# Two single banks in place of a joint pair for the experts, a bank's copy on VectorE, and three moves in a hand-written order

## The chip, the core and the metric

One core of a Trainium2 chip runs the whole program. The metric is device time in microseconds (us), the median of several executions. TensorE (PE) does the matrix products and writes them to PSUM, which has eight banks of 128 x 512 fp32; VectorE (DVE), ScalarE (ACT) and GpSimd (POOL) work on the results, and SyncE (SP) issues most of the loads. Each engine takes its instructions strictly in program order, and waits between engines go over semaphores.

## The reference

Attention over 8 batches, 8 heads, 576 positions of 64 (fp32, scores masked by blocks of 64 rows), and a mixture of 8 experts on its output, one expert per token:

```
scores = q @ k.T / 8, masked by blocks;  x = softmax(scores) @ v          # 4608 tokens x 512
logits = x @ w_gate + modality_bias[modality_id];  e = argmax(logits)
out[token] = softmax(logits)[e] * (relu(x[token] @ w1[e]) @ w2[e])        # w1 512x1024, w2 1024x512
```

## The kernel before

**Attention** works on pairs of heads, 32 pairs, four pairs to a batch. `run_slot` walks a table of names, `ORDER`, once for each pair: at slot p, `S0` to `S3` write the scores of pair p+1 (L216), `M0` to `M4` take negated row maxima on VectorE (L220), `E0` to `E4` the exponentials on ScalarE (L226), `T0` to `T2` transpose the exponentials of pair p on PE (L235), `C0` to `C4` copy the transposes from PSUM to the tile `pt` (L249, all on ScalarE), `G` and `H` make the gate's columns (L255, L258), `V` multiplies with the values of pair p-1 (L281), and `D`, `Z0`, `Z1` divide (L296 to L310, VectorE). So the order of every engine's queue is written out by hand, in ORDER; nothing reorders it later.

Scores and transposes use six banks: `bank0` to `bank3` and the two halves of `wide`, one PSUM tile of 1024 columns (`banks[4]`, `banks[5]`); its last row block of scores spans both. The value products go to `o0` and `b0`. Waits are placed by the tile framework from the tiles that instructions read and write; for `wide` one tile name stands for both banks.

**Routing** of a batch starts in the slot after its fourth pair: a list of about 20 small steps (`logits` to `place_sum`, mostly VectorE on 128x72) is popped by the names `q1` to `q6`, `qp` and `qv` in ORDER. Then nine scatters (L406, GpSimd) write the batch's records to DRAM, a VectorE instruction (L405) each.

**The last slot** follows its own table, `LAST`, which mixes the last pair's `V`, `D`, `Z` and the last routing with the first expert products: `+turn0` transposes fetched rows, `+up0` to `+up3` are the first eight products with w1, `+place` issues one scatter behind a pause of POOL (L642), and `+flush` all that are left.

**Experts** then run in blocks of 512 rows: eight `up` products (L754, 128x512 each from 12 matmuls; evicted by L757 on ScalarE and L758 on VectorE into `hidden`, an upper and a lower part), with the first half of the `down` products behind the fourth and the second half at the end (L855). A block has four down results `y`, one per bank of `ys`; `finish` (L862, ScalarE) scales one and a GpSimd scatter writes it out (L863):

```
ys = (o0, banks[5], banks[4], b0)
if nxt is not None:
    (self.turn_third if nxt.parts == THIRD else self.turn_rows)(nxt)
...
for i in range(s.parts):
    self.down(s, i, range(4, 8) if s.parts == WIDE else range(8))
```

`turn_rows` transposes the next block's rows on VectorE (L738), rounds them on ScalarE (L741) and takes the remainder on VectorE (L744, L745). It stands ahead of the second half of the down products, so on ScalarE its four casts are queued ahead of the four `finish` instructions.

Of the kernel before, what the change touches and what calls it, by code (L numbers as in the profile page):

```python
# [11 lines left out]
F32 = mybir.dt.float32  # L12
# [7 lines left out]
PSUM = bass.MemoryType.PSUM  # L20
DRAM = bass.MemoryType.DRAM

B, H, S, D = 8, 8, 576, 64
N, DM, NE, DF = 4608, 512, 8, 1024
NPAIR = B * H // 2
# [39 lines left out]
    ((7, 0), (7, 1), (7, 2), (7, 3)), ((8, 0), (8, 1), (8, 2), (8, 3)), ((6, 3), (4, 2), (2, 1)),  # L65
)
POS = {x: 4 * r + i for r, room in enumerate(ROOMS) for i, x in enumerate(room)}
SUMS = ((2, 4, 6, 5), (1, 3, 7, 8, 0))
TAILS = ((6, 3, 20, 0), (0, 5, 20, 1), (4, 2, 21, 0), (8, 4, 21, 1), (2, 1, 22, 0))
PRODUCTS = tuple(((s,), j) for j in range(4) for s in (6, 7, 5, 8, 4, 3, 2, 1) if s >= 2 * j + 1)  # L70
# [1 line left out]
PARTS = (("idf", (128,)), ("ii", (128,)), ("iom8", (NE,)), ("iom72", (NSUB, NE)), ("first9", (NE, NSUB)), ("base8", (NE,)), ("edges", (N // SLOT,)), ("side", (NSUB,)), ("token", (NSUB,)), ("nth", (N // 128,)), ("few", (2,)), ("half", (1,)))  # L72

ORDER = (
# [3 lines left out]
)  # L78
OPENING = ("S0", "S1", "S2", "S3", "M0", "E0", "M1", "E1", "M2", "E2", "M3", "E3", "M4", "E4")
WARM = {"T1": 3}  # L80
# [4 lines left out]
    (18, "V"): ("chosen", "stage"), (18, "T1"): ("stage",), **{(slot, "T1"): ("restage",) for slot in range(19, 32)}, (20, "L"): ("ids",), (26, "T0"): ("fetch",), (31, "T0"): ("fetch",),  # L85
}
LAST = (
    ("+turn0", 0), ("V", 1), ("+place", 0), ("D", 1), ("+up0", 0), ("+place", 0), ("Z0", 1), ("Z1", 1), ("+steps1", 0), ("+place", 0), ("+up1", 0),
    ("+place", 0), ("+steps10", 0), ("+place", 0), ("+up2", 0), ("+place", 0), ("+steps9", 0), ("+up3", 0), ("+flush", 0),
)  # L90

# [21 lines left out]
def attention_moe(ctx, tc, qk, vr, bkw, mid, mb, w1, w2, cf, ld, out):  # L113
    nc = tc.nc
    pe, act, dve, pool = nc.tensor, nc.scalar, nc.vector, nc.gpsimd

    cst = ctx.enter_context(tc.tile_pool(name="cst", bufs=1, side="left"))
    drm = ctx.enter_context(tc.tile_pool(name="drm", bufs=1, space=DRAM))
    records = drm.tile([2 * NROW, REC], F32, name="records")

    cft = cst.tile([128, cf.shape[1]], F32, name="cf")
    con, off = {}, 0
    for n, shape in PARTS:
        size = int(np.prod(shape))
        v = cft[:, off : off + size]
        con[n] = v.rearrange("p (a b) -> p a b", a=shape[0]) if len(shape) > 1 else v
        off += size
    idf, ii, iom8, iom72, first9, base8, side, token = (con[n] for n in ("idf", "ii", "iom8", "iom72", "first9", "base8", "side", "token"))
    wg = cst.tile([128, PPB, 2 * NE], F32, name="wg")
    scratch = cst.tile([128, 1024], F32, name="scratch")  # L130
# [4 lines left out]
    run = cst.tile([128, NE], F32, name="run")  # L135
# [1 line left out]
    midf = cst.tile([128, 2, B * NSUB], F32, name="midf")  # L137
    mbt = cst.tile([128, 2, NE], F32, name="mbt")
    bias = cst.tile([128, B * NSUB, NE], F32, name="bias")
    cst.tile([128, 32], F32, name="padc")  # L140
    steady = ctx.enter_context(tc.tile_pool(name="steady", bufs=1, side="left"))
    extra = steady.tile([128, 14 * 1024], F32R, name="extra")
    staging = [steady.tile([128, 1024], F32, name=f"staging{i}") for i in range(2)]
    xg0 = steady.tile([128, 1024], F32, name="xg0")
# [9 lines left out]
    ps = ctx.enter_context(tc.tile_pool(name="ps", bufs=1, space=PSUM))  # L154

    banks = [ps.tile([128, 512], F32, name=f"bank{i}") for i in range(4)]
    wide = ps.tile([128, 1024], F32, name="wide")
    banks += [wide[:, 0:512], wide[:, 512:1024]]
    o0, b0 = (ps.tile([128, 512], F32, name=n) for n in ("o0", "b0"))
    xrb.append(att.tile([128, NSUB, REC], F32, name="xr2"))  # L160
    btmp = staging[0][:, 0 : B * NSUB * NE].rearrange("p (a e) -> p a e", e=NE)
    raws = [att.tile([128, 2 * S], F32, name=f"raw{i}") for i in range(2)]
# [74 lines left out]
    def copies(p, c):  # L237
        g, h = c // 2, c % 2
        n = len(GROUPS[g])
        first = min(POS[x] for x in GROUPS[g])  # L240
        if g == 2:
            dst = pairs[p].pt[:, first : first + n].rearrange("p b (h q) -> p h b q", h=2)
            src = wide.rearrange("p (h c) -> p h c", h=2)[:, :, 0 : 64 * n].rearrange("p h (b q) -> p h b q", q=64)
        else:
            dst, src = pairs[p].pt[:, first : first + n, 64 * h : 64 * h + 64], banks[c][:, 0 : 64 * n].rearrange("p (b q) -> p b q", q=64)
        if g == 0:
            dst = pairs[p].pt[:, 0:16, 64 * h : 64 * h + 64].rearrange("p (a b) q -> p a b q", b=4)[:, 0:4:3]
            src = src.rearrange("p (a b) q -> p a b q", a=2)
        act.copy(dst, src)  # L249

    def gates(p):
        for j in range(6):
# [61 lines left out]
    def routing(b):  # L314
# [97 lines left out]

            placing.extend((scatter, i) for i in range(NSUB))

        return [logits, total, total_out, biased, top, shifted, hits, expo, hit_index, first, onehot, counts, weight, counts_out, running, place_run, place_pick, weight_guard, weight_out, place_sum]

    sel = {}

# [81 lines left out]
    def run_slot(slot):  # L500
        nonlocal steps, ex
        for name, stage in LAST if slot == NPAIR else ORDER:
            p = slot - stage
            if placing and slot < NPAIR and name in SPOTS:
                g, c = placing.pop(0)
                g(c)
            for what in EARLY_STEPS.get((slot, name), ()):
                if ex is None:
                    ex = Experts(ctx, tc, cst, scratch, con["edges"], con["nth"], con["few"], con["half"], records, early_reads, scatters, bias, rest, bases, idf, w1, w2, out, sel, run, base8, pick, dot, banks, (o0, banks[5], banks[4], b0), placing, staging, extra, firsts, first, xrb, xg0, pts[0][:, 15:19], lambda kind: any(getattr(f, "kind", "") == kind for f in steps))
                ex.early(what)  # L510
            if name[0:6] == "+steps":
                for f in steps[0 : int(name[6:])]:
                    f()
                steps = steps[int(name[6:]) :]
                continue
            if slot == 0 and name in WARM:
                warm(WARM[name])
            if name[0] == "+":
                ex.early(name[1:])
                continue  # L520
            if name[0] == "q":
                kind = "" if name[1].isdigit() else name
                kinds = (kind,) if kind else ("", "c")
                quick = bool(steps) and getattr(steps[0], "kind", "") == "c"
                for _ in range(1 if kind else 2 * (name != "q6") if quick else 2 if slot in HURRIED else 1 + (len(steps) > 20)):
                    if slot > 1 and steps and getattr(steps[0], "kind", "") in kinds:
                        steps.pop(0)()
                continue
            if not 0 <= p < NPAIR and name not in ("L", "v", "Y"):
                continue  # L530
            if p < NPAIR:
                emit(name, p)
            if name == "Z1" and p % PPB == PPB - 1:
                these = routing(p // PPB)
                steps = these[0:1] + steps + these[1:]
                if p // PPB == EARLY - 1:
                    choose(Later(dve, steps))

    engines = {ET.PE, ET.Activation, ET.DVE, ET.Pool}
    with tc.manual_schedule(engines=engines | {ET.SP}):  # L540
        load(0)
        for _ in range(NWARM):
            pe.matmul(b0, zeros[:, 0:128], zeros, start=True, stop=True)
        nc.sync.dma_start(cft, cf)
        load(1)
        scale(0)
        load_rest()
        for name in OPENING:
            emit(name, 0)
        for slot in range(NPAIR + 1):  # L550
            run_slot(slot)
    with tc.manual_schedule(engines=engines):
        att_stack.close()
        ex.run_all(steps)
# [493 lines left out]
```

## Time and profile before

| | |
|---|---|
| median of 3 runs | 736.71 us (736.17 to 738.45) |
| profiled execution | 742.5 us, its span 740.6 us |
| PE busy | 702.5 us, 95% of the span |
| DVE, ACT, POOL busy | 331.6, 337.3, 216.5 us |
| attention (32 pairs) | to about 293 us of the span |
| expert blocks | from there to the end |

An engine's busy share is an average over both stages. A busy PE is one that has instructions in flight; a gap of it is idle time, and the view names what ended the gap. "granted clock" (PEclk) is the share of TensorE's 2.4 GHz that it was given.

### The profile page before, as it was taken

The page shows a single profiled execution, that of the slowest core. Times are in us where ns is not written, and L with a number is a line of the kernel's source. Part 1 is how long each engine was busy: PE and PEld are TensorE (multiplying, and loading weights), DVE is VectorE, ACT ScalarE, POOL GpSimd, SP SyncE. Part 2 cuts the span into 40 slices and gives each one's busy share as a digit, 9 for nine tenths or more (in the row PEclk, how much of TensorE's full clock was granted, in tenths as well). Part 3 has the DMA queues.
Part 4 walks back from the last instruction along what each step waited for, and adds up shares of the span by engine and source line. Part 5 has one row for each costly group of instructions (what it writes and reads, how often), then busy time and mean ns, then how long its engine had stood idle before and what let it go on. Part 6 is the DMA issues. An engine that isn't in the chain of part 4 may idle for free. (4 is left out here: it accounts for less than half of the span.)

```text
span 740.6 us, 20776 instructions
## 1 busy us (share of the span) xinstructions
PE 702.5 (95%) x8618; PEld 578.5 (78%) x8619; DVE 331.6 (45%) x974; ACT 337.3 (46%) x673; POOL 216.5 (29%) x251
## 2 busy tenths in 40 slices
PE   8999999999999998999599899898999999999996
PEld 5888888788878887888478788787887878878785
DVE  4665767776777786752312322223122132222121
ACT  6888887778888886221221221213113032131211
POOL 2422253545275763799020110201002010020111
PEclk9999999999999999999889999999999999999999
DMA  6555565667676865231741420403407030020100
GB/s 211 168 156 162 170 188 178 192 195 237 192 248 201 274 210 152 60 136 54 144 114 58 85 67 19 114 1 77 149 0 228 1 81 33 0 79 1 50 32 24
DMA packets 52690, 87.78 MB, mean 119 GB/s; under 512 B 10350, under 2 KB 31086, under 8 KB 52592
## 3 DMA queue, kind: packets, MB, share of 16 engines
q1 hardware_dynamic: 46064, 66.90, 33.0%
q0 software_dynamic: 6528, 19.50, 7.3%
q8 instruction: 69, 1.13, 0.6%
q14 instruction: 29, 0.24, 0.1%
HBM read 65.28 MB, written 21.27 MB: 117 GB/s over the span
## 5 line engine op out<-in xcount | busy, mean ns | idle before, releaser
L758 DVE SCALAR_TENSOR_TENSOR extra<-bank,extra 128x512 fp32r<-128x512 f32 (+1 forms) x70 | 46.8, 669 | 263.4 <-ACT extra L757 263.4
L757 ACT ACTIVATE extra<-bank 128x512 fp32r<-128x512 f32 (+1 forms) x70 | 40.7, 581 | 219.6 <-PE bank L754 219.6
L220 DVE TENSOR_REDUCE nm<-bank 128x1 f32<-128x512 f32 (+2 forms) x192 | 85.5, 484 | 62.8 <-PE bank L216 56.5
L406 POOL DMA_INDIRECT records<-xr,pi x72 | 73.5, 1020 | 115.3 <-DVE den L296 47.9
L226 ACT ACTIVATE pm<-bank,nm 128x512 f32<-128x512 f32 (+2 forms) x192 | 91.6, 527 | 27.6 <-DVE nm L220 24.0
L281 PE MATMUL b<-v,pt 64*64 64x73 f32 (+1 forms) x1612 | 97.8, 227 | 0.0
L281 PE MATMUL o<-v,pt 64*64 64x73 f32 (+1 forms) x1488 | 93.5, 228 | 0.3 <-issue 0.3
L216 PE MATMUL bank<-raw 64*64 64x64 f32 (+5 forms) x768 | 93.0, 442 | 0.4 <-DMA raw<-qk 0.4
L281 PEld LDWEIGHTS o<-v,pt 64*64 64x64 f32 (+1 forms) x1488 | 81.6, 135 | 13.1 <-issue 6.5
L281 PEld LDWEIGHTS b<-v,pt 64*64 64x64 f32 (+1 forms) x1612 | 85.1, 136 | 0.2 <-issue 0.2
L249 ACT COPY pt<-bank 128x512 f32<-128x512 f32 x128 | 66.3, 605 | 9.9 <-PE bank L235 8.8
L855 PE MATMUL wide<-extra 128*128 128x512 f32 x216 | 55.5, 412 | 15.4 <-ACT scratch L862 15.4
L855 PEld LDWEIGHTS wide<-extra 128*128 128x128 f32 x216 | 42.6, 199 | 26.2 <-ACT scratch L862 17.1
L216 PE MATMUL wide<-raw 64*64 64x64 f32 (+3 forms) x512 | 58.9, 369 | 1.0 <-ACT pt L249 0.9
L754 PE MATMUL bank<-extra,w0ha 128*128 128x512 f32 (+1 forms) x176 | 59.0, 361 | 0.0
L863 POOL DMA_INDIRECT out<-scratch,ids_b x9 | 8.8, 974 | 164.5 <-ACT scratch L862 163.6
L754 PE MATMUL bank<-extra,w0la 128*128 128x512 f32 (+1 forms) x152 | 56.6, 372 | 0.0
L226 ACT ACTIVATE pm<-wide,nm 128x256 f32<-128x256 f32 (+2 forms) x96 | 43.8, 527 | 20.3 <-DVE nm L220 14.9
L855 PE MATMUL wide<-w1b,extra 128*128 128x512 f32 x192 | 47.0, 397 | 5.9 <-ACT scratch L862 5.9
L754 PE MATMUL bank<-xtl,w0ha 128*128 128x512 f32 x128 | 50.6, 395 | 0.0
L754 PE MATMUL bank<-extra,w0lb 128*128 128x512 f32 x128 | 50.3, 393 | 0.0
L754 PE MATMUL bank<-extra,w0hb 128*128 128x512 f32 x128 | 50.1, 391 | 0.0
(241 smaller groups left out, 1234.7 us busy)
## 6 DMA issues: line engine op xcount, KB each, us to landing
raw<-qk SPq DMA_DIRECT2D x31, 576.0 KB
v<-vr SPq DMA_DIRECT2D x32, 438.0 KB
vt<-qk SPq DMA_DIRECT2D x32, 288.0 KB
xr<-records SPq DMA_DIRECT2D x32, 256.0 KB
staging<-w SPq DMA_DIRECT2D x32, 128.0 KB
staging<-w SPq DMA_DIRECT2D x8, 512.0 KB
plain<-w SPq DMA_DIRECT2D x16, 128.0 KB
plain<-w SPq DMA_DIRECT2D x4, 512.0 KB
```

Source lines behind the costliest of these rows:

```text
L216: pe.matmul(place(s, a, b)[64 * t : 64 * t + 64], d.q[hs, D * s : D * s + D], d.k[hs, a:b], start=True, stop=True)
L220: dve.tensor_reduce(pairs[p].nm[:, s : s + 1], whole(s), AX.X, ALU.max, negate=True)
L226: act.activation(d.pm[:, o : o + D * (s + 1)], whole(s), AF.Exp, bias=d.nm[:, s : s + 1], scale=1.0)
L249: act.copy(dst, src)
L281: pe.matmul(o, d.pt[rows, at, t : t + 64], d.v[rows, h, block, :], start=key not in begun, stop=last)
L406: last = pool.indirect_dma_start(records[:], bass.IndirectOffsetOnAxis(ap=g.pi[i], axis=0), xr[:, i, :], None, bounds_check=2 * NROW - 1, ...
L754: nc.tensor.matmul(hp, w[:, kc, ms], x[:, kc, 0:n], start=i == 0, stop=i == len(mm) - 1)
L757: nc.scalar.activation(hh, hp, AF.Relu)
L758: nc.vector.scalar_tensor_tensor(hl, hp, 0.0, hh, ALU.max, ALU.subtract)
L855: nc.tensor.matmul(y, s.hs[m][x][:, ts], self.part(w, 1, m // 2)[:, m % 2, :], start=first, stop=last)
L863: last = nc.gpsimd.indirect_dma_start(self.out, bass.IndirectOffsetOnAxis(ap=s.list.ids[:, s.t + i : s.t + i + 1], axis=0), yo, None, boun ...
```

## The change

Six edits. The pool that holds `wide` is closed ahead of the last slot, and two tiles of one bank each, `late0` and `late1`, take its place in `banks[4:6]` and in the experts' `ys`. The copy `C1` (bank 1) goes to VectorE. In ORDER, `C1` stands directly behind `C0`, `q2` ahead of `qp`, and `q3` to `q6` behind `E4` (before, `q2` to `q5` stood between the maxima). In the routing list `counts_out` stands ahead of `weight`. In LAST, `+up0` stands ahead of `V`. An unused tile `padc` of 128 x 32 is dropped. Numbers of lines and of tiles differ between the two programs for that reason.

```diff
-    ("Q", -1), ("L", -2), ("V", 1), ("v", -1), ("D", 1), ("Z0", 1), ("Z1", 1), ("T0", 0), ("C0", 0), ("T1", 0), ("C2", 0), ("C1", 0), ("C3", 0),
+    ("Q", -1), ("L", -2), ("V", 1), ("v", -1), ("D", 1), ("Z0", 1), ("Z1", 1), ("T0", 0), ("C0", 0), ("C1", 0), ("T1", 0), ("C2", 0), ("C3", 0),
...
-    ("+turn0", 0), ("V", 1), ("+place", 0), ("D", 1), ("+up0", 0), ("+place", 0), ("Z0", 1), ("Z1", 1), ("+steps1", 0), ("+place", 0), ("+up1", 0),
+    ("+turn0", 0), ("+up0", 0), ("+place", 0), ("V", 1), ("+place", 0), ("D", 1), ("Z0", 1), ("Z1", 1), ("+steps1", 0), ("+place", 0), ("+up1", 0),
...
+    o0, b0 = (ps.tile([128, 512], F32, name=n) for n in ("o0", "b0"))
+    joint = ExitStack()
+    wide = joint.enter_context(tc.tile_pool(name="joint", bufs=1, space=PSUM)).tile([128, 1024], F32, name="wide")
...
-        act.copy(dst, src)
+        dve.tensor_copy(dst, src) if c in ON_DVE else act.copy(dst, src)
...
-        for slot in range(NPAIR + 1):
+        for slot in range(NPAIR):
             run_slot(slot)
+        joint.close()
+        late = ctx.enter_context(tc.tile_pool(name="late", bufs=1, space=PSUM, reuse_waits="tile"))
+        banks[4:6] = [late.tile([128, 512], F32, name=f"late{i}") for i in range(2)]
+        ex.ys = (o0, banks[5], banks[4], b0)
+        run_slot(NPAIR)
```

`ON_DVE` is `(1,)`. On PE, at the second half of the down products of the first block of 512 rows, with the engines that a row waits for in brackets, there stood

```order
L855 MATMUL o_101<-extra 128x512 [waits DVE_49]
L855 MATMUL wide<-extra 128x512 x12
L855 MATMUL wide<-extra 128x512 [waits Activation_49]
L855 MATMUL wide<-extra 128x512 x11
L855 MATMUL b_102<-extra 128x512 x12
```

and now stands

```order
L861 MATMUL o_99<-extra 128x512
L861 MATMUL o_99<-extra 128x512 [waits DVE_49]
L861 MATMUL late_6149<-extra 128x512 x12
L861 MATMUL late_6148<-extra 128x512 x12
L861 MATMUL b_100<-extra 128x512 x12
```

The wait for ScalarE between the second and the third result is no longer there. On VectorE, in a slot of the first batch's routing (`nm` are the maxima), there stood

```order
L310 TENSOR_TENSOR gl<-o_101,inv 128x32
L220 TENSOR_REDUCE nm<-bank_96 128x1
L220 TENSOR_REDUCE nm<-bank_98 128x1 x2
L383 SCALAR_TENSOR_TENSOR cum<-cf,table 128x72
L385 TENSOR_TENSOR pos<-table,run 128x72
L220 TENSOR_REDUCE nm<-bank_97 128x1 x2
L394 TENSOR_TENSOR eq<-cum,pos 128x72
L220 TENSOR_REDUCE nm<-bank_99 128x1
L397 TENSOR_TENSOR eq<-eq,oh 128x72
L398 TENSOR_TENSOR run<-run,cum 128x8
L220 TENSOR_REDUCE nm<-wide 128x1 x3
L380 TENSOR_SCALAR sm<-sm 128x9
```

and the same steps, one slot earlier, now stand behind all maxima, with the new copy ahead of these:

```order
L250 COPY pt_113<-bank_96 128x2x4x64
L221 TENSOR_REDUCE nm<-bank_95 128x1
L221 TENSOR_REDUCE nm<-bank_97 128x1 x2
L221 TENSOR_REDUCE nm<-bank_96 128x1 x2
L221 TENSOR_REDUCE nm<-bank_98 128x1
L221 TENSOR_REDUCE nm<-wide 128x1 x3
L378 TENSOR_REDUCE sm<-ex 128x9
L384 SCALAR_TENSOR_TENSOR cum<-cf,table 128x72
L386 TENSOR_TENSOR pos<-table,run 128x72
L395 TENSOR_TENSOR eq<-cum,pos 128x72
L398 TENSOR_TENSOR eq<-eq,oh 128x72
L399 TENSOR_TENSOR run<-run,cum 128x8
```

The third place is PE at the start of the last slot. The last pair's value products (L281) followed the gate's (b_102) there:

```order
L255 MATMUL b_102<-wg,vt 64x16 x11
L281 MATMUL bank_96<-v_108,pt_112 64x73 [waits DMAHW1_49,Activation_49]
L281 MATMUL bank_96<-v_108,pt_112 64x73
L281 MATMUL bank_97<-v_108,pt_112 64x73 x2
L281 MATMUL bank_96<-v_108,pt_112 64x73 x2
```

Now the products of `+up0` do, which wait for the turned rows, and the value products stand behind them:

```order
L256 MATMUL b_100<-wg,vt 64x16 x11
L760 MATMUL bank_97<-extra,w0ha 128x256 [waits Activation_49,Pool_49]
L760 MATMUL bank_97<-extra,w0la 128x256 [waits Pool_49]
L760 MATMUL bank_97<-extra,w0ha 128x256 [waits DVE_49]
L760 MATMUL bank_97<-extra,w0ha 128x256 [waits Pool_49]
```

What moved there is a whole product group: 24 matmuls with w1 now precede 100 value products. On POOL, the program of before has 18 pauses of L642 and the changed one 12, since the routing of a batch comes to its scatters a slot earlier.

## Rows read from the trace of the kernel before

**Rows 1.** The page: busy time, share of the span and instructions of engines.

```profile
PE 702.5 (95%) x8618; PEld 578.5 (78%) x8619; DVE 331.6 (45%) x974; ACT 337.3 (46%) x673; POOL 216.5 (29%) x251
```

**Rows 2.** Waits, longest first: us in total, times, longest us.

```profile
PE wide L855 <- ACT scratch L862: 21.4, 8, 9.9
```

**Rows 3.** Second to fourth down result: us, PE busy (matmuls), PEclk, DMA share, GB/s.

```profile
358.35:376.37 18.02, 8.16 (x25) 0.72 0.97 186
414.73:423.68 8.95, 7.09 (x26) 0.84 0.64 111
...
693.19:699.82 6.63, 5.85 (x26) 1.00 0.38 121
sum 71.53, PE 50.15; mean PE 6.27
```

**Rows 4.** The same windows at two first halves, undisturbed.

```profile
392.87:398.31 5.44, 5.44 (x26) 1.00 0.64 193
532.24:537.83 5.59, 5.59 (x26) 1.00 0.00 0
```

**Rows 5.** Timeline of the first block of 512 rows: start, us, engine, line.

```profile
357.08 2.03 SPq L725 DMA_DIRECT2D xr<-records  x4
...
365.06 1.30 DVE L738 STREAM_TRANSPOSE xr<-xr 128x512 f32<-128x512 f32 x2 [7.91 <-DMA xr<-records]
...
369.90 0.69 DVE L745 TENSOR_TENSOR xtl<-xr,extra 128x512 fp32r<-128x512 f32 x1
370.36 0.68 ACT L862 ACTIVATE scratch<-wide,both_lead 128x512 f32<-128x512 f32 x1
...
371.09 5.47 PE L855 MATMUL wide<-extra 128*128 128x512 f32 x12 [9.86 <-ACT scratch L862]
```

**Rows 6.** Timeline of POOL and SP ahead of that load: last scatters, then lists.

```profile
348.06 1.53 POOL L642 TENSOR_SCALAR pt<-pt 128x512 f32<-128x512 f32 x1
349.77 1.03 POOL L406 DMA_INDIRECT records<-xr,pi  x1 [0.18 <-issue]
352.28 0.42 SPq L700 DMA_DIRECT2D both_a<-records  x1
```

**Rows 7.** Windows of 4, 13, 13 pairs and one: us, then PE, PEld, DVE, ACT, POOL busy.

```profile
13.20:47.78 34.58, 34.58 (x847) 29.41 (x843) 21.95 (x66) 28.84 (x63) 12.43 (x11) 1.00 0.53 158
47.78:164.62 116.84, 113.84 (x2744) 96.31 (x2743) 82.39 (x309) 94.59 (x205) 43.40 (x39) 1.00 0.59 178
164.62:282.89 118.27, 115.93 (x2745) 97.22 (x2745) 87.90 (x306) 96.05 (x209) 65.17 (x100) 1.00 0.72 222
47.78:55.97 8.19, 8.19 (x211) 7.10 (x211) 6.02 (x21) 6.82 (x17) 1.36 (x2) 1.00 0.51 153
```

**Rows 8.** Lines by form, 13.2 to 282.89 us: busy, mean ns, idle before.

```profile
L249 ACT COPY pt<-bank 128x512 f32<-128x512 f32 x122 | 63.3, 605 | 9.5 <-PE bank L235 8.4 <-PE wide L235 1.1
...
L216 PEld LDWEIGHTS wide<-raw 64*64 64x64 f32 x480 | 24.3, 133 | 11.5 <-ACT pt L249 8.0
...
L220 DVE TENSOR_REDUCE nm<-bank 128x1 f32<-128x512 f32 x30 | 20.7, 692 | 57.2 <-PE bank L216 51.6 <-ACT table L337 4.0 <-PE b L255 1.6
...
L226 ACT ACTIVATE pm<-wide,nm 128x256 f32<-128x256 f32 x30 | 14.3, 476 | 19.4 <-DVE nm L220 14.3 <-DVE pi L405 1.3 <-DVE xr L391 1.0
```

**Rows 9.** Windows on PE at the last slot, and one pair's value products.

```profile
293.25:298.17 4.92, 4.92 (x101) 0.65 1.12 228
276.32:279.64 3.32, 3.32 (x104) 1.00 0.13 47
291.25:311.87 20.62, 17.41 (x209) 0.92 0.37 86
```

**Rows 10.** Timeline of PE in the last slot.

```profile
293.25 4.92 PE L281 MATMUL bank<-v,pt 64*64 64x73 f32 x100 [1.80 <-ACT v L258]
...
304.10 0.39 PE L754 MATMUL wide<-extra,w0ha 128*128 128x256 f32 x1 [1.41 <-DVE extra L758]
```

**Rows 11.** Window on VectorE over one pair's division (D, Z0, Z1).

```profile
207.01:208.57 1.56, 1.49 (x10) 1.00 0.43 88
```

More of the change, by code (lines that the diff above doesn't have):

```diff
@@ L67 @@
 POS = {x: 4 * r + i for r, room in enumerate(ROOMS) for i, x in enumerate(room)}
+ON_DVE = (1,)
 SUMS = ((2, 4, 6, 5), (1, 3, 7, 8, 0))
@@ L139, in attention_moe @@
     bias = cst.tile([128, B * NSUB, NE], F32, name="bias")
-    cst.tile([128, 32], F32, name="padc")
     steady = ctx.enter_context(tc.tile_pool(name="steady", bufs=1, side="left"))
@@ L156, in attention_moe @@
     banks = [ps.tile([128, 512], F32, name=f"bank{i}") for i in range(4)]
-    wide = ps.tile([128, 1024], F32, name="wide")
+    o0, b0 = (ps.tile([128, 512], F32, name=n) for n in ("o0", "b0"))
+    joint = ExitStack()
+    wide = joint.enter_context(tc.tile_pool(name="joint", bufs=1, space=PSUM)).tile([128, 1024], F32, name="wide")
     banks += [wide[:, 0:512], wide[:, 512:1024]]
-    o0, b0 = (ps.tile([128, 512], F32, name=n) for n in ("o0", "b0"))
     xrb.append(att.tile([128, NSUB, REC], F32, name="xr2"))
@@ L413, in place_sum @@
             placing.extend((scatter, i) for i in range(NSUB))
-        return [logits, total, total_out, biased, top, shifted, hits, expo, hit_index, first, onehot, counts, weight, counts_out, running, place_run, place_pick, weight_guard, weight_out, place_sum]
+        return [logits, total, total_out, biased, top, shifted, hits, expo, hit_index, first, onehot, counts, counts_out, weight, running, place_run, place_pick, weight_guard, weight_out, place_sum]
     sel = {}
@@ L508, in run_slot @@
                 if ex is None:
-                    ex = Experts(ctx, tc, cst, scratch, con["edges"], con["nth"], con["few"], con["half"], records, early_reads, scatters, bias, rest, bases, idf, w1, w2, out, sel, run, base8, pick, dot, banks, (o0, banks[5], banks[4], b0), placing, staging, extra, firsts, first, xrb, xg0, pts[0][:, 15:19], lambda kind: any(getattr(f, "kind", "") == kind for f in steps))
+                    ex = Experts(ctx, tc, cst, scratch, con["edges"], con["nth"], con["few"], con["half"], records, early_reads, scatters, bias, rest, bases, idf, w1, w2, out, sel, run, base8, pick, dot, banks, (), placing, staging, extra, firsts, first, xrb, xg0, pts[0][:, 15:19], lambda kind: any(getattr(f, "kind", "") == kind for f in steps))
                 ex.early(what)
```

4 rows, old and new, of the table ORDER are left out of this document.

## The prediction

> **What bounds the kernel now.** I read the page first: PE is busy for 95% of the span, no other engine for half of it [rows 1]. So two things can shorten the program: gaps of PE, and stretches in which it is busy but paced by others. Next the waits: the longest of PE is one kind, products into `wide` that wait for ScalarE's L862, 21.4 us in 8 times, the longest 9.9 [rows 2]. Eight is the number of 512-row blocks, so I measured each of them over windows, from the start of the second down result to the start of the fourth [rows 3]. The eight windows hold 71.53 us. In a first half, where nothing stalls, the same two results take 5.44 us with the first expert's weights and 5.59 us with the second's [rows 4]; four blocks are of either kind, 44.1 us. The excess is **27.4 us**: 12.6 in the first block, 3.5 in the second, about 2 in each of five, 1.0 in the last. It is more than the 21.4 us of idle time, because the granted clock is 0.72 and 0.84 in the first two windows: after a gap PE goes on at 1.2 GHz for a while.
>
> The timeline of the first block shows why PE waits. L862 reads the second result, in one half of `wide`; the third result goes to the other half. The tile framework sees one tile, and lets the third wait for the read of the second. ScalarE comes to that read late, since the four casts of the next block's rows are queued ahead of it, and these wait for rows that land at 365.06: the read starts at 370.36, PE goes on at 371.09 [rows 5]. Nothing in the data asks for that wait.
>
> **The change part by part.**
>
> *Two tiles for the joint pair.* With `late0` and `late1` the third result has no wait in the program's order, nor has the fourth. What is late next? After the fourth result PE needs the next block's turned rows and a bank for the next up product. In the six middle blocks the rows are turned while PE is still in the down products, so nothing replaces the stall. In the first block PE would be through with the fourth result at 358.35 + 2 x 5.44/2 + 2.72 = 366.5, and the turning ends at 369.90 + 0.69 = 370.6 [rows 5]; the first up product, of 12 matmuls in the order of the four parts, would end some 4 us late. But the rows come earlier too. The load at 357.08 follows the lists' loads (352.28), and these the last scatter of POOL at 349.77, the end of a row of 18 pauses of 1.53 us with a scatter of 1.03 each, 2.8 us a step [rows 6]. Only 12 are left in the changed program, so this row could end 6 x 2.8 = 17 us earlier; since the last batch's own nine cannot start before its routing, I take 11. Rows that land near 354 are turned in the shadow of the down products. I take the whole 27.4 us; at the worst, with rows no earlier, 23.4. The last slot has the same false wait once more, 1.41 us at 304.10 [rows 10]; it is in that slot's term.
>
> *The attention pairs.* From score product to score product, 30 pairs take 34.58 + 116.84 + 118.27 = 269.69 us: 8.65 us a pair in the first four, before any routing, 8.99 in the next thirteen and 9.10 in the last thirteen [rows 7]. PE's busy share is 97 to 100%, yet the shortest pair takes 8.19 us with the same products [rows 7]. So PE is busy and paced: matmuls stand in flight behind semaphores. Two rows say which. The loads of scores into `wide` wait for ScalarE's copies 8.0 us, and the exponentials wait for maxima, 14.3 us at `wide`'s alone [rows 8].
>
> (a) C1 to VectorE takes 605 ns [rows 8] from ScalarE's chain C0, C2, C1, C3, C4, so `wide` comes free about 0.5 us earlier; that covers the wait just named (0.27 us a pair), and PE gains no more than it waits. (b) The routing steps behind the maxima let the last exponentials start earlier by the two to five steps that stood between. (c) The copy costs VectorE between ScalarE's 605 ns and its own read of 512 columns, 692 ns [rows 8]; I take 0.69, since that is the same engine and the same bank width. It waits for C0, and lies in the gap ahead of the first maximum, 57.2 us in 30 pairs or 1.9 a pair [rows 8]. Behind the copy queue q1, q2 and that maximum. Without this cover it would cost 0.69 x 30 = 21 us, the lower bound of this term; the upper bound is all pairs at 8.19, 269.69 - 245.7 = 24 us gained.
>
> Between the two I go by VectorE's budget. It is busy 82.39/13 = 6.3 us a pair in the middle stretch and 87.90/13 = 6.8 in the last, where it also scales q [rows 7]; with the copy 7.0 and 7.5. What it must wait for stays: the first maximum for its scores (1.9 less the copy, 1.2). That makes 8.2 and 8.7, plus some 0.2 in pairs where four to six routing steps now stand ahead of the division, which waits for nothing else then, and which gates wait for. I take 8.3, 8.45 and 8.8 us a pair: 34.58 - 33.2 = 1.4, 116.84 - 109.9 = 7.0, 118.27 - 114.4 = 3.9, together **12.2 us**.
>
> The Trainium skill speaks against moving the copy: the page "VectorE: DVE Perf Modes", section "Specifications", places ScalarE closer to PSUM and VectorE closer to SBUF, and its table of op costs ("The TRN2 errata") would make a copy of 512 columns from PSUM an estimated 0.66 us on VectorE against 0.57 on ScalarE. The rows above have the same sign with 692 against 605 ns, and by the page's price the lower bound would be 20 us in place of 21.
>
> *The last slot.* PE waited 1.80 us there, then ran the value products in 4.92 us where another pair's took 3.32, since the granted clock was 0.65, then waited 1.41 us [rows 9, 10]. Now 24 up products stand first. They need rows that VectorE turns behind the previous pair's division, the copy and two scatter indices, so I expect PE to wait about as long, and the lower clock to hit the up products in place of the values. The second wait, 1.41 us, goes. From the gate's end to the first down result it is 20.62 us [rows 9]; I take **1 us** gained, from 3 lost to 5 gained. `counts_out` ahead of `weight` changes the order of two steps of 0.2 to 0.4 us, off PE's path; the dropped tile costs nothing.
>
> **The sum.** 27.4 + 12.2 + 1 = 40.6 us. Against the profiled execution's 742.5 us this makes 702; that execution is 5.8 us above the median, and I take the same gain from the median: 736.7 - 40.6 = **696 us**.
>
> **The rivals.**
>
> *Every pair at its floor.* VectorE's added work is all hidden and each pair takes 8.19 us: 27.4 + 24 + 1, 684 us. For it: in the shortest pair VectorE is busy for only 6.02 of the 8.19 us [rows 7]. Against it: VectorE is idle only 1.65 us a pair in the last stretch once the copy is in.
>
> *VectorE becomes the bound of attention.* The copy and the routing tails land on the division, which gates and the bank's release wait for; the pairs take as long as before or up to 0.69 us more: 708 to 729 us. For it: VectorE's 7.5 us of work in a pair with two fixed waits. Against it: its own gap ahead of the maxima.
>
> *The wait for `wide` only moves*, to rows not yet turned in the first block, and later reads of `late` wait as `wide` did: only attention and the last slot gain, 723 us. The program's order speaks against it, for no row of the third result waits.
>
> *Slower.* The copy stands behind the whole division, 1.56 us [rows 11], which waits for the value products; scores into bank 1 wait for the copy, and the next value products for the scores. If that ring closes, a pair costs the division and the copy more, 1.56 + 0.69 us, 67.5 us in 30 pairs: 736.7 - 28.4 + 67.5 = 776 us. It decides from 28.4/30 = 0.95 us a pair on. Against it: scores reach bank 1 last but one of their pieces, and the division ends before they start.
>
> **How the numbers follow.** The sum has a chance of 0.52 (its own range 690 to 704), every pair at its floor 0.15, VectorE as the bound 0.25, the moved wait 0.03, slower 0.03; 0.02 for no change by mishaps that cancel. I leave out the far end of VectorE's case and the last three: 684 to 713 us. No change means within 0.3%, 2.2 us, about what a measurement of this kernel can tell: 0.02. Slower 0.03, faster 0.95.
>
> **What would show it.** In the changed profile PE has no wait for L862 in the down products, and windows from the second to the fourth result hold 5.44 and 5.59 us with the granted clock at 1.00, also in the first block. The last scatter comes 10 us or more earlier against the first down result. A pair takes 8.3 to 8.8 us; the copy takes 0.6 to 0.7 us on VectorE, and exponentials wait less for maxima. In the last slot PE waits ahead of `+up0`. The prediction is wrong if the pairs' average stays at 9 us or falls to 8.2, or if PE waits for turned rows behind the fourth result.

## The result, and the profile after

The changed kernel takes **699.09 us** (median of 4 runs, 697.74 to 699.53) against 736.59 before (4 runs, 736.17 to 738.45): a ratio of 0.9483, 95% interval 0.9462 to 0.9504, 37.5 us gained. Its profiled execution took 697.74 us, with a span of 695.9. PE is now busy for 97% of it; the row answers to [rows 1]:

```profile
PE 677.0 (97%) x8619; PEld 573.5 (82%) x8619; DVE 350.3 (50%) x1006; ACT 318.6 (46%) x641; POOL 206.9 (30%) x245
```

The waits of PE in the changed kernel, longest first (us in total, times, longest), have none for the `finish` line, which is L868 now:

```profile
PE b L256 <- DVE gl L311: 3.3, 7, 1.0
PE o L374 <- DVE oh L370: 2.8, 3, 1.2
PE o L334 <- DVE l L331: 2.4, 7, 0.7
PE bank L760 <- ACT extra L747: 1.5, 1, 1.5
```

Windows of the changed kernel, with the columns of [rows 7]: the 4, 13 and 13 pairs; the last six of these pairs; the last slot from the gate's end to the first down result; second to fourth down result in the first, the second, the fifth (the first of the second expert) and the last block of 512 rows; and the whole expert part.

```profile
12.98:46.06 33.08, 32.85 (x846) 28.64 (x843) 24.22 (x70) 26.97 (x59) 12.66 (x11) 1.00 0.56 167
46.06:154.83 108.77, 107.02 (x2744) 94.58 (x2743) 89.63 (x327) 86.82 (x193) 44.38 (x39) 1.00 0.65 192
154.83:271.45 116.62, 109.51 (x2749) 97.00 (x2745) 97.05 (x328) 88.66 (x194) 68.66 (x102) 0.99 0.78 230
214.69:271.45 56.76, 51.51 (x1268) 45.47 (x1267) 46.00 (x158) 40.87 (x91) 37.72 (x56) 0.97 0.74 225
279.59:299.03 19.44, 17.32 (x201) 16.52 (x201) 13.51 (x40) 5.96 (x16) 11.72 (x11) 0.91 0.22 65
345.30:350.74 5.44, 5.44 (x25) 4.50 (x24) 3.97 (x7) 3.08 (x6) 0.97 (x1) 1.00 0.25 65
388.82:394.26 5.44, 5.44 (x25) 4.50 (x24) 3.96 (x7) 3.08 (x6) 0.55 (x1) 1.00 0.24 61
...
519.38:524.82 5.44, 5.44 (x25) 4.50 (x24) 3.96 (x7) 3.07 (x6) 0.97 (x1) 1.00 0.27 64
...
649.94:655.38 5.44, 5.44 (x25) 4.50 (x24) 0.00 (x0) 1.37 (x2) 1.94 (x2) 1.00 0.34 99
299.03:690.17 391.14, 390.79 (x1762) 323.90 (x1760) 113.91 (x206) 96.44 (x157) 62.49 (x69) 1.00 0.27 71
```

All eight windows of down results hold 5.44 us, where [rows 3] have 18.02 to 6.63, and the clock is 1.00 in each. The expert part takes 391.1 us; before, from the first down result at 311.87 to the start of the last matmul at 734.93, it took 423.1. Pairs take 8.27, 8.37 and 8.97 us.

The timeline of the changed kernel in the last slot and at the first block of 512 rows answers to [rows 5, 6, 10]. The last scatter of records starts at 322.45, 23.4 us behind the first down result; before, it was 37.9 us behind it. The next rows' load follows at 330.08, the turning starts at 344.02 with no wait for a DMA, and the third result does not wait while ScalarE reads the second (349.31):

```profile
281.10 0.35 PE L760 MATMUL bank<-extra,w0ha 128*128 128x256 f32 x1 [1.51 <-ACT extra L747]
...
286.14 3.29 PE L282 MATMUL bank<-v,pt 64*64 64x73 f32 x100
289.36 0.39 PE L760 MATMUL late<-extra,w0ha 128*128 128x256 f32 x1
...
322.45 1.03 POOL L407 DMA_INDIRECT records<-xr,pi  x1 [0.18 <-DVE extra L764]
...
330.08 2.04 SPq L731 DMA_DIRECT2D xr<-records  x4
...
344.02 1.29 DVE L744 STREAM_TRANSPOSE xr<-xr 128x512 f32<-128x512 f32 x2
345.30 5.60 PE L861 MATMUL late<-extra 128*128 128x512 f32 x24
...
349.31 0.68 ACT L868 ACTIVATE scratch<-late,both_lead 128x512 f32<-128x512 f32 x1
```

Three groups by form over the 30 pairs (busy us, mean ns, idle before) answer to [rows 8]. The score loads into `wide` hardly wait any more (0.6 us, before 11.5); the first exponentials of `wide` find 9.8 us of idle time, 9.2 of it for maxima, before 19.4 and 14.3; the copy on VectorE takes 681 ns.

```profile
L217 PEld LDWEIGHTS wide<-raw 64*64 64x64 f32 x480 | 25.0, 137 | 0.6
...
L227 ACT ACTIVATE pm<-wide,nm 128x256 f32<-128x256 f32 x30 | 14.2, 474 | 9.8 <-DVE nm L221 9.2 <-DVE ei_a L105 0.3 <-DVE di_a L105 0.3
...
L250 DVE COPY pt<-bank 128x512 f32<-128x512 f32 x30 | 20.4, 681 | 0.0
```

Over all exponentials of the 30 pairs, though, the waits of ScalarE for maxima have grown, from 32.3 us before (first row) to 47.9 (second row; us in total, times, longest). The growth stands ahead of the largest exponential of one bank (38.5 us of idle time, before 13.6); that ScalarE comes to it sooner, with one copy less to make, fits but is not shown.

```profile
ACT pm L226 <- DVE nm L220: 32.3, 57, 1.3
...
ACT pm L227 <- DVE nm L221: 47.9, 59, 2.4
```

### The profile page after: what moved, and what is told of

Read it like the earlier page. It is cut to its first block, busy times and chain, and to the rows that moved or that the text cites. A ratio compares the mean times of both kernels' runs of the same rounds, so it can differ in the third digit from the quotient of the medians.

```text
span 695.9 us, 20802 instructions
## 1 busy us (share of the span) xinstructions
PE 677.0 (97%) x8619; PEld 573.5 (82%) x8619; DVE 350.3 (50%) x1006; ACT 318.6 (46%) x641; POOL 206.9 (30%) x245
## 5 line engine op out<-in xcount | busy, mean ns | idle before, releaser
L227 ACT ACTIVATE pm<-bank,nm 128x512 f32<-128x512 f32 (+2 forms) x192 | 87.3, 529 | 46.4 <-DVE nm L221 45.0
L221 DVE TENSOR_REDUCE nm<-bank 128x1 f32<-128x512 f32 (+2 forms) x192 | 81.2, 483 | 41.2 <-PE bank L217 41.0
L282 PE MATMUL b<-v,pt 64*64 64x73 f32 (+1 forms) x1612 | 94.6, 226 | 0.0
L282 PE MATMUL o<-v,pt 64*64 64x73 f32 (+1 forms) x1488 | 90.0, 228 | 0.0
L282 PEld LDWEIGHTS o<-v,pt 64*64 64x64 f32 (+1 forms) x1488 | 78.4, 135 | 12.1 <-issue 6.9
L217 PE MATMUL bank<-raw 64*64 64x64 f32 (+5 forms) x768 | 88.3, 446 | 0.0
L217 PEld LDWEIGHTS bank<-raw 64*64 64x64 f32 x768 | 41.6, 135 | 12.8 <-issue 7.1
L250 ACT COPY pt<-bank 128x512 f32<-128x512 f32 x96 | 50.1, 595 | 3.4 <-PE bank L236 2.2
L861 PE MATMUL late<-extra 128*128 128x512 f32 x216 | 50.4, 389 | 0.0
L760 PE MATMUL bank<-xtl,w0hb 128*128 128x512 f32 x128 | 49.8, 389 | 0.0
```

Source lines behind the costliest of these rows:

```text
L217: pe.matmul(place(s, a, b)[64 * t : 64 * t + 64], d.q[hs, D * s : D * s + D], d.k[hs, a:b], start=True, stop=True)
L221: dve.tensor_reduce(pairs[p].nm[:, s : s + 1], whole(s), AX.X, ALU.max, negate=True)
L227: act.activation(d.pm[:, o : o + D * (s + 1)], whole(s), AF.Exp, bias=d.nm[:, s : s + 1], scale=1.0)
L250: dve.tensor_copy(dst, src) if c in ON_DVE else act.copy(dst, src)
L282: pe.matmul(o, d.pt[rows, at, t : t + 64], d.v[rows, h, block, :], start=key not in begun, stop=last)
L760: nc.tensor.matmul(hp, w[:, kc, ms], x[:, kc, 0:n], start=i == 0, stop=i == len(mm) - 1)
```

## The experiments

The kernel before took 737.66 us beside the first four kernels, 737.23 beside the next four, and 743.53 on the chip of the last four; there, ratios are compared. Windows have the columns above. "Attention" is 30 pairs, from score product to score product.

### The two tiles alone

The kernel before with the joint pool, `late0` and `late1`, and nothing else:

```diff
+        joint.close()
+        late = ctx.enter_context(tc.tile_pool(name="late", bufs=1, space=PSUM, reuse_waits="tile"))
+        banks[4:6] = [late.tile([128, 512], F32, name=f"late{i}") for i in range(2)]
+        ex.ys = (o0, banks[5], banks[4], b0)
```

> The kernel before with the two single tiles alone (pad, orders and copies as before). If the false wait was the cause, PE has no wait for L862's successor in the down products. The load of the first 512-row block's successor is no earlier here, so PE should wait some 4 us for turned rows behind that block's fourth result: 27.4 - 4 us of stalls and 1.4 us in the last slot gone, 711 to 712 us. If the whole 27.4 us go whatever the scatters do, 708 us. If the wait only moves, 723 us or more. Products that read one operand from either end of SBUF should keep their slower pace, 0.232 us from start to start.

Measured: 710.69 us, ratio 0.9626 [0.9604, 0.9648], 27.0 us of the 37.5. In its trace the second and third result of the first block take 5.44 us, but what follows, the fourth result and the next block's up products to the first half of its down products, takes 16.66 us, where the next block has 13.71:

```profile
353.76:359.20 5.44, 5.44 (x26) 4.51 (x25) 0.00 (x0) 0.00 (x0) 0.00 (x0) 1.00 1.13 199
359.20:375.86 16.66, 14.96 (x62) 10.88 (x61) 7.34 (x11) 6.45 (x11) 1.96 (x2) 1.00 0.68 140
384.06:397.77 13.71, 13.71 (x62) 11.27 (x61) 2.07 (x3) 1.80 (x3) 2.17 (x6) 1.00 0.08 29
```

So the false wait (the third result waiting for a read of the other half of `wide`) was the cause of the stall, and the rows are what is late next: here the last scatter is still 37.8 us behind the first down result, and PE waits for turned rows. This costs 16.66 - 13.71 = 2.95 us. The expert part of this trace takes 398.3 us, 24.8 less than the 423.1 of before; some 2 us of the 27.0 that the medians give are not located. In its last slot the false wait is gone, too, but PE waits 1.6 us for a step of the late routing in its place, and the slot takes 19.97 us, as it does in the kernel before without `padc` (287.43 to 307.40 and 285.20 to 305.17).

### The unused tile

`padc` dropped from the kernel before, kept in the changed one, and kept there with 64 and with 16 columns:

```diff
-    cst.tile([128, 32], F32, name="padc")
```

> The kernel before without the unused tile of 32 columns, nothing else. The prediction called it worth nothing: 736.6 us. The rival: the tile shifts all that lies behind it at the left end of SBUF by 128 bytes a partition against the tiles at the right end, and matmuls that take one operand from either end run 0.232 us instead of 0.227: some 770 of 512 columns, 4 to 5 us, so 732 us, with all expert matmuls at 0.227.

> The changed kernel with the unused tile of 32 columns put back. By the prediction 699 us, no change. By the rival that the tile's place sets the matmuls' pace, 4 to 5 us more, 703 to 704 us, and 0.232 us from start to start for the second expert's down products.

> The changed kernel with an unused tile of 64 columns (256 bytes of each partition) where before had 32 (128 bytes). If what counts for the pace of matmuls is the place of one operand against the other within 256 bytes or less, all 512-column matmuls keep 0.227 us and the time is 699 us; if any shift of the left end costs it, those with one operand at either end take 0.232 us as with 32 columns and the time is 702 to 703 us.

> The changed kernel with an unused tile of 16 columns (64 bytes of each partition). 256 bytes cost nothing (698.8 us, all matmuls at 0.227 us), 128 bytes cost 3.7 us (702.8). If the place within 256 bytes counts: 702 to 703 us, pace 0.23 us or more for operands at either end; if only a place within 64 bytes counts in another way, 699 us.

Measured: 736.0 us (0.9977 [0.9963, 0.9992]) for before without it; 702.84 us (0.9528 [0.9504, 0.9551]) for the changed kernel with it; 698.77 us (0.9482 [0.9463, 0.9501]) with 64 columns; 0.9549 [0.9526, 0.9571] with 16. The starts of successive matmuls with 512 columns show where the time goes. With 128 bytes of padding they are 0.232 us apart where `w1b` meets `extra` and 0.234 where `xtl` meets `w0ha`; without padding and with 256 bytes all are 0.226 to 0.227 apart, and with 64 bytes many are 0.228 to 0.233 (means over 96 to 216 matmuls each). `xtl` and `w1b` are allocated from the right end of SBUF and `extra` from the left, where `padc` shifted all tiles behind it. Products with both operands from one end keep 0.226 to 0.227 us with 128 bytes; with 64 bytes some of these are slower, too (`xtl` with `w0hb` 0.233). The expert part of the changed kernel grows by 4.13 us with 32 columns of padding, the first row (compare 391.14); two results of the second expert take 5.58 us again, the second row:

```profile
299.87:695.14 395.27, 394.92 (x1762) 324.06 (x1760) 113.91 (x206) 96.50 (x157) 61.55 (x69) 1.00 0.27 70
...
499.37:504.95 5.58, 5.58 (x26) 4.52 (x25) 0.00 (x0) 0.00 (x0) 0.00 (x0) 1.00 0.00 0
```

In the kernel before the same pace gained next to nothing: in its trace three of the stalls grew by 1.4 to 1.6 us. Four of its windows from second to fourth result, without `padc`: PE is idle for 1.86 us in the last three, and yet the granted clock is 1.00 in one of them and 0.81 in two, which are 1.6 us longer. All eight sum to 76.00, where [rows 3] have 71.53.

```profile
351.31:369.07 17.76, 7.79 (x26) 5.98 (x25) 5.26 (x8) 3.61 (x6) 0.98 (x1) 0.71 0.98 182
...
454.47:462.06 7.59, 5.73 (x26) 4.42 (x25) 4.10 (x7) 3.20 (x6) 2.09 (x2) 1.00 0.50 94
500.14:509.34 9.20, 7.34 (x26) 5.59 (x25) 4.10 (x7) 3.21 (x6) 2.08 (x2) 0.81 0.64 110
547.45:556.64 9.19, 7.33 (x26) 5.58 (x25) 4.10 (x7) 3.20 (x6) 1.94 (x2) 0.81 0.64 111
...
13.47:276.78 263.31, 260.66 (x6332) 221.26 (x6328) 191.62 (x681) 217.78 (x472) 121.24 (x148) 1.00 0.66 199
```

The last row is its attention, which is that of the kernel before: 263.3 us, not 269.7 as in [rows 7]. I come back to it below.

### Attention alone

The kernel before with the copy on VectorE, the new ORDER and the list's new order; `wide`, LAST and `padc` as before:

> The kernel before with the copy on VectorE, the new ORDER and counts_out ahead of weight; joint pair, pad and last slot as before. The pairs should take what they take in the changed kernel, 11 us less. Routing ends a slot earlier, so six pauses fewer stand in POOL's row and the load of the first block's successor comes over 10 us earlier; then that block's stall shrinks from 12.6 to 2 to 4 us although the false wait stays: together 715 to 717 us. If the scatters' row has no part in that stall, 725 us.

Measured: 723.27 us, ratio 0.9811 [0.9778, 0.9844]. Attention takes 259.3 us (13.27 to 272.60), and the last scatter comes at +23.4 us. With the rows on time the window of the first block, from the second to the fourth result, is 7.59 us where [rows 3] have 18.02; the eight windows sum to 62.9 us:

```profile
346.35:353.94 7.59, 5.73 (x26) 4.42 (x25) 4.09 (x7) 3.19 (x6) 0.97 (x1) 1.00 0.50 94
```

So the false wait costs 18.8 us even with early rows (62.9 - 44.1), and the scatters' shorter row took 8.6 us off it, net of two windows at a granted clock of 0.81. My expectation of 715 to 717 was too low because it put attention's gain at 11 us; it is about 4.

### The copy

Bank 1's copy back on ScalarE, in its old place, in the changed kernel; and the same in a version of it with single routing steps (next section):

```diff
-ON_DVE = (1,)
+ON_DVE = ()
...
-    ... ("T0", 0), ("C0", 0), ("C1", 0), ("T1", 0), ("C2", 0), ("C3", 0),
+    ... ("T0", 0), ("C0", 0), ("T1", 0), ("C2", 0), ("C1", 0), ("C3", 0),
```

> The changed kernel (699.1 us) with bank 1's copy back on ScalarE and back in its old place; all else as changed. Theory (the copy shortens ScalarE's chain, so that the joint pair of banks comes free earlier): the first four pairs, which have no routing, go back from 8.1 to about 8.5 us, and the others lose 0.2 to 0.4 us each as well, 6 to 10 us in 30 pairs: 705 to 709 us. Rival (the routing steps' new place carries attention's gain, the copy next to nothing): only the first pairs are longer, and the last dozen, where VectorE has most to do, are up to 0.7 us shorter without the copy: 696 to 701 us.

> The kernel of 692.2 us (two steps for a name in slot 30 only) with bank 1's copy back on ScalarE, in its old place. Theory (the copy on VectorE gains in every pair what it gains in the first four, 0.4 us, since VectorE's own work is covered once the double steps are gone): 30 pairs lose 0.2 to 0.4 us: 698 to 704 us. Rival (the copy matters little; it was 3 us with the double steps): 693 to 696 us.

Measured: 702.16 us (0.9517 [0.9496, 0.9537]), 3 us above the changed kernel (the intervals touch, but its fastest run, 700.41 us, is above the changed kernel's slowest); and 0.9537 [0.9514, 0.9559] against 0.9400 for the version with single steps, 10 us; there attention takes 269.3 us, against 260.4 in the version with both edits (below) on the same chip. The first row has the first four pairs of the former, 34.56 us: as long as before [rows 7], to 0.02 us.

```profile
13.11:47.67 34.56, 34.56 (x847) 29.42 (x843) 21.95 (x66) 28.79 (x63) 12.47 (x11) 1.00 0.54 158
13.11:276.97 263.86, 256.28 (x6332) 221.15 (x6329) 196.89 (x695) 217.25 (x474) 125.96 (x152) 0.99 0.68 202
```

So in pairs without routing the copy alone makes the whole gain, 0.37 us a pair. In the last six pairs, where the double steps of the next section stand, the changed kernel is shorter without the copy (54.19 us against 56.76); so 702.16 lies between the two expectations. With the copy on ScalarE the 30 pairs take 263.9 us, no less than the kernel before without `padc` (263.3): moving the routing steps, as it stands, gains nothing in attention in sum. In the middle 13 pairs it gains 3.4 us (110.91 against 114.34), in the last 13 it loses 4.0 (118.39 against 114.42).

### Routing steps

Two edits of the changed kernel. `HURRIED` lists the slots in which a name of ORDER pops two routing steps; and the steps back between the maxima, in the old order:

```diff
-HURRIED = (25, 26, 29, 30, 31)
+HURRIED = (30,)
```

```diff
-    ("q2", 1), ("qp", 1), ... ("M1", -1), ("E1", -1), ... ("E4", -1), ("q3", 1), ("q4", 1), ("q5", 1), ("q6", 1),
+    ("qp", 1), ... ("M1", -1), ("q2", 1), ("E1", -1), ("M2", -1), ("q3", 1), ... ("E4", -1), ("q6", 1),
```

> The changed kernel with two routing steps for each name in slot 30 alone, not in slots 25, 26, 29 and 31. Theory (two steps for a name, now in a row behind the maxima, are what makes the last pairs longer than before: they stand ahead of the division, for which the gates wait): the pairs of 9.75, 9.21, 9.89 us come down by 0.5 to 1 us each, 2 to 4 us in all: 695 to 697 us. Rival (the routing that comes later pushes its scatters and the last slot back, so that the first down result comes no earlier): 699 to 702 us.

> The changed kernel with the routing steps back between the maxima, and the two steps of the list in their old order; the copy on VectorE, the two late tiles, the last slot and the dropped tile as changed. Theory (steps behind the maxima gain in pairs with single steps and lose as much in the last pairs with double steps, where they stand in a row ahead of the division): pairs 5 to 24 longer by 0.2 to 0.4 us, pairs 25 to 30 shorter by 0.5 to 1 us each, so 698 to 703 us in all, and the scatters of the last batches later. Rival (the steps' place is what gains in attention): 704 to 708 us.

Measured: **692.18 us** (690.92 to 694.72), ratio 0.9400 [0.9379, 0.9421], with single steps: 7 us less than the changed kernel (6.1 by the ratios), and more than the 2 to 4 us that I expected. The middle 13 pairs are as long as there (108.76), and the last six take 50.50 us in place of 56.76:

```profile
46.19:154.95 108.76, 107.02 (x2744) 94.53 (x2743) 89.63 (x327) 86.83 (x193) 44.39 (x39) 1.00 0.64 192
154.95:264.71 109.76, 107.47 (x2748) 95.56 (x2744) 94.18 (x317) 87.64 (x193) 65.49 (x99) 1.00 0.78 239
214.21:264.71 50.50, 49.48 (x1267) 44.01 (x1266) 43.72 (x147) 39.93 (x90) 34.53 (x53) 1.00 0.78 241
```

The double steps, now in one row ahead of the division, cost the last six pairs 6.3 us. In these pairs of the changed kernel PE waits 4.5 us for VectorE, 1.3 of it at the gates behind the division and 3.2 at products of the routing itself; with single steps 0.8 us are left. A part of the 6.3 us is the granted clock, 0.97 over the six pairs and 1.00 with single steps. With single steps the last scatter comes at +29.1 us, and the expert part still takes 391.1.

With the steps back between the maxima the ratio is 0.9562 [0.954, 0.9583], 5.8 us above the changed kernel by the ratios. Attention is no longer in sum: 262.46 us, against 264.87 in the run with 16 columns of padding, whose order of attention is that of the changed kernel, on the same chip. In its parts the theory held: the middle 13 pairs take 2.8 us more with the steps between the maxima (first row; third row with 16 columns of padding), 0.2 us a pair, and the last 13 take 5.2 us less (second row; fourth row), 3.3 of it in the last six.

```profile
46.51:160.57 114.06, 111.06 (x2744) 96.73 (x2743) 89.25 (x322) 87.63 (x191) 42.66 (x38) 1.00 0.61 182
160.57:275.88 115.31, 112.31 (x2746) 97.44 (x2745) 95.77 (x319) 89.27 (x195) 65.23 (x99) 1.00 0.76 227
...
45.89:157.13 111.24, 109.38 (x2743) 95.96 (x2743) 90.78 (x329) 86.91 (x191) 44.34 (x39) 1.00 0.63 189
157.13:277.68 120.55, 113.39 (x2746) 98.79 (x2744) 97.68 (x326) 89.99 (x196) 68.78 (x102) 0.99 0.75 222
```

The loss of the whole stands behind attention, in the last slot and in the expert part:

```profile
13.42:275.88 262.46, 256.23 (x6333) 222.78 (x6329) 209.15 (x711) 203.89 (x442) 120.55 (x147) 1.00 0.67 200
284.71:307.20 22.49, 17.75 (x200) 17.11 (x201) 14.87 (x50) 6.05 (x17) 13.06 (x11) 0.85 0.35 79
307.20:702.70 395.50, 393.39 (x1762) 324.65 (x1760) 115.23 (x212) 96.04 (x157) 75.36 (x80) 1.00 0.28 72
```

Its waits on PE in the last slot say how: VectorE still has eight instructions of the last routing ahead of the rows that `+up0` needs.

```profile
PE bank L760 <- ACT extra L747: 4.7, 1, 4.7
```

And the last scatter is back at +37.9 us, so PE waits for turned rows behind the fourth result of the first block: 395.50 - 391.14 = 4.4 us, of which 1.8 are idle time and the rest slower products behind it. So the move of the routing steps buys earlier rows, and 0.2 to 0.3 us in each of the middle pairs, with single steps; in the pairs with double steps it loses more than that.

### The last slot

The value products ahead of the first up products again, in the changed kernel and in the one with single steps:

```diff
-    ("+turn0", 0), ("+up0", 0), ("+place", 0), ("V", 1), ("+place", 0), ("D", 1), ...
+    ("+turn0", 0), ("V", 1), ("+place", 0), ("D", 1), ("+up0", 0), ("+place", 0), ...
```

> The changed kernel with the value products ahead of the first up products in the last slot, as before. Theory (the order of the two only decides which of them meets the lower clock; the gain of the last slot is the false wait of 1.4 us on the joint pair, which stays gone): 698 to 700 us, the last slot from the gate's end to the first down result within 1 us of the 19.65 us of the changed kernel. Rival (the up products in front are what gains): 700.5 to 702 us, that stretch 21 us or longer.

> The changed kernel with both edits that were faster alone: two routing steps for a name in slot 30 only (692.2 us alone) and the value products ahead of the first up products in the last slot (696.3 us alone, its last slot 1.6 us shorter in the profile, 2.8 us by the medians). Theory (the two are independent): 689 to 691 us. Rival (the last slot is paced by the last routing, which now comes later, so that the order of products there is without effect): 692 us.

Measured: 696.3 us (693.61 to 702.03, ratio 0.9453 [0.9421, 0.9485]) and, with single steps, 0.9400 [0.9378, 0.9423], the ratio of single steps alone. In both traces the last slot is shorter, 17.84 us against 19.44 and 17.51 against 18.92, and the granted clock in it is 1.00, not 0.91. Both expectations for the first missed this: the slot is shorter, not as long or longer. The window of the changed kernel with values first:

```profile
279.78:297.62 17.84, 15.46 (x201) 15.10 (x201) 12.63 (x40) 5.87 (x16) 11.74 (x11) 1.00 0.23 68
```

Attention and the last slot of the version with both edits:

```profile
12.71:273.13 260.42, 255.22 (x6333) 222.16 (x6329) 211.16 (x713) 202.14 (x441) 122.79 (x150) 1.00 0.69 202
281.82:299.33 17.51, 15.91 (x201) 15.46 (x201) 11.90 (x46) 6.04 (x16) 13.26 (x12) 1.00 0.40 91
```

The difference of some 1.5 us goes with the granted clock, and the order alone does not decide the clock. The version of the section on the copy that has single steps and the copy on ScalarE has `+up0` in front, too, and PE waits 1.6 us ahead of it; yet its clock stays at 1.00, and its last slot is as short:

```profile
291.33:309.05 17.72, 15.93 (x201) 15.27 (x201) 12.05 (x40) 5.98 (x17) 14.20 (x12) 1.00 0.35 84
```

In the kernel before, on the other hand, the value products stood in front and the clock fell (0.65 over them, [rows 9]). The first kernel's ratio is lower than that of the changed kernel, but the intervals overlap; the second's shows no difference from single steps alone, as the rival said. So it is not shown that either order is the faster one.

## Why the prediction was right, and where it was not

The forecast was faster, 696 us, with 684 to 713 as its range; it is 699.1. The mechanisms of the false wait and of the copy were right. Two terms were mis-sized, the dropped tile by 4.1 us and attention by 7.4, and they partly cancel: that the sum came within 3.1 us is in part luck.

**The false wait (27.4 us).** Right: removed alone it gained 27.0 us, and together with the earlier rows the expert part went from 423.1 to 395.3 us with `padc` kept, 27.8. That the rows come earlier was needed for the whole of it, and was shown both ways: with late rows 2.95 and 4.4 us are lost, where I had put 4 at the worst. The scatters came 14.5 us earlier against the first down result; I had taken 11.

**The dropped tile ("costs nothing").** This step failed. It is worth 4.1 us of the expert part: with its 128 bytes, matmuls with one operand from either end of SBUF are slower. I had seen 5.44 and 5.59 us in [rows 4] and taken the second for a property of the second expert's weights; in the changed kernel both are 5.44.

**Attention (12.2 us).** Mis-sized, and by the base more than by the pairs: the forecast's values sum to 257.5 us, and 258.47 was measured. In the two profiles it is 269.69 - 258.47 = 11.2 us. But the profiled execution of before lay 5.8 us above the median, and I took "the same gain from the median". That excess sat in attention: in two other runs with the same order of attention, the tiles alone and the dropped tile alone, the first 26 of the pairs take 228.27 and 227.99 us, and in [rows 7]'s execution 232.90. Against 263.3 us the gain is 4.8. Of the single values, 8.3 and 8.45 us a pair were close (8.27, 8.37); 8.8 for the last pairs was too low (8.97), since I gave the double steps in a row only 0.2 us, and they cost 6.3 us in the last six pairs. The rival in which VectorE becomes the bound is borne out in these six pairs alone (56.76 us, where the kernel before without `padc` has 53.52), and VectorE's budget of 8.7 us was no floor: with single steps the last 13 pairs take 8.44 us with VectorE busy for 7.2. Mechanism (b), the new place of the routing steps, holds for single steps, 0.2 to 0.3 us a pair, and turns into a loss with double steps; in sum it gave attention nothing. One sign did not come: exponentials wait less for maxima ahead of `wide`, but more in all, 47.9 us for 32.3.

**The copy.** It takes 0.681 us on VectorE and 0.595 on ScalarE in the changed kernel; I had 0.69. The Trainium skill, "VectorE: DVE Perf Modes", section "The TRN2 errata", has a table of op costs that makes it an estimated 0.66 and 0.57 us: the trace agrees within 5%. The slower copy is still the better place, for it lies in a gap of VectorE and off ScalarE's chain; the wait of scores for `wide`, 8.0 us in [rows 8], is gone. Where no routing stands in the way it gains 0.37 us a pair, more than the 0.27 that I took as the most, since I let PE gain only what it was seen to wait.

**The last slot (1 us).** Right in its sum: the forecast's window, from the start of the last gate product, went from 20.62 to 19.65 us, and the stretch from the last pair's scores to the first down result from 28.4 (before without `padc`) to 27.6. It was right, too, that the low clock would hit the up products: the 24 take 5.04 us (281.10 to 286.14) at a granted clock of 0.66, the values 3.29. But where the clock did not fall and the false wait is gone the slot takes 17.5 to 17.8 us in either order, so the order of products is not what gained. The false wait is, once the routing comes early: with it, and the clock at 1.00, the kernel with the attention edits alone takes 19.25 us (280.74 to 299.99).

The sum by these measurements: 27.8 + 4.1 + 4.8 + 0.8 = 37.5 us, the difference of the medians. That it fits to the tenth is chance: the terms are read from single executions, and with the attention of 259.4 us, which the kernel with `padc` kept and the one with the attention edits alone have beside 263.3 us, the third term would be 3.9.

## What to carry to other kernels

A PSUM tile over two banks is one thing to the waits: where the two banks have different lives, give each a tile. Before a sum is made against a profiled execution that lies off the median, find the stage where the excess sits, or the gain of that stage is counted too high. Work that is moved off one chain is queued in another: look at the slots where the most of it lands, here the pairs with two steps for a name.

## What the runs showed of the hardware

An unused tile of 128 bytes in each partition made matmuls of 512 columns with one operand from either end of SBUF 2 to 3% slower (0.227 to 0.232 and 0.234 us), 64 bytes did too (expert part 396.9 us in place of 391.1), 256 bytes not at all; why the offset counts was not tested further. A gap of 1.86 us on PE was followed by a granted clock of 1.00 in some blocks and 0.81 in others of one execution, and a gap of 1.5 us in the last slot by 0.66 over the next 5.04 us, where one of 1.6 us in another kernel left it at 1.00. And attention took longer on one chip than on another where the expert part did not: the version with both edits took 260.4 us for its 30 pairs where single steps alone, of the same order there, took 251.6 on another chip, and 391.1 us for the experts on both. What lengthens the pairs there, from the eighth on, and what did in the profiled execution of before, stays open.
